# Moving up to three heads' columns of V in each weighted-sum matmul of a windowed attention

## The chip, the cores and the metric

The kernel runs on one core of one Trainium2 chip. The metric is the device time of one execution in microseconds (us), lower is better. A run's time is a little longer than the span of its profile, which reaches from the first to the last instruction.

## What is computed

The reference mixes two branches of a sequence of 2048 positions and 640 channels by a gate: a convolution as long as the sequence (done by FFT in the reference, by matmuls with constant matrices in the kernel), and an attention of 32 heads of 20 channels, where each position looks at 8 positions, 2 apart. The change lies in the last but one line of the attention:

```
x = A_q
g = _sigmoid((x * gate_w).sum(-1, keepdims=True))
a = _A_ref(x, A_k, A_v, A_shift_k, A_ssm_k, A_ssm_D)     # the long convolution
# _B_ref, the attention:
qkv = (x @ wqkv).reshape(B, S, 3, H, Dh)                  # H = 32, Dh = 20
idx = pos[:, None] - 2 * arange(8)[None, :]               # masked where idx < 0
logits = einsum("bhsd,bhswd->bhsw", q, kg) * scale
attn = softmax(logits)
o = einsum("bhsw,bhswd->bhsd", attn, vg)
return o.reshape(B, S, D) @ wo
# the result: g * a + (1 - g) * b
```

## The kernel before, in words

The sequence is split into even and odd positions, so that a window is 8 neighbours, and each half into 9 blocks of 114 queries, 18 blocks in all; a block's queries need 121 keys. The 32 heads are worked in 8 sets `t` of 4 heads. For one set there are these steps:

- `score_gen` (matmuls on L595, tile `sc`): for each block and head one matmul gives keys x queries, 121 x 114. A head's weights hold 31 rows, in one quarter of the array's rows, and two heads at a time stand in different quarters. The blocks are taken in five groups (4, 4, 4, 3, 3 blocks), each in two steps `k` of two heads, so a set has 10 steps, of 8 or 6 matmuls.
- ACT makes the exponentials of a step in one instruction (L602) and writes them to `ETall`, a ring of 8 buffers.
- `pv_gen` (L623, tile `O`): for each block and head the 121 x 128 block of `ETall` is loaded as weights and 21 columns of `VW` are moved through it: the 20 channels of V for that head and a column of ones, which gives the softmax's sum. A set has 72 such matmuls, 48 for the first 12 blocks and 24 for the last 6, each of the two parts in one go after all its exponentials. Within a part the loops run over groups, then heads (`hf`, `hh`), then blocks, so the four heads `h4 = 0..3` of a block follow one another in time. The results of the four heads of a block stand side by side in PSUM, 84 columns a block, 21 a head.
- DVE divides (L632, L635) into `oS`.

`VW` holds for each block all 32 heads side by side, 21 columns each, so neighbouring heads are neighbours in memory.

Around it, other work shares TensorE (PE) in an order that is written out by hand: the strings ORDER and ENGINES name, request by request, which generator issues next and whether ACT or DVE evicts. Four PSUM buffers of two banks go round. The projection of V (L478, all rows of the array, 320 columns) comes first and makes `VW`. Up to about 107 us the projections of Q and K (`pj`, L527, all rows, 342 or 349 columns) fill the places between the scores. After that the FFT's first steps on the filter do (`s1_unit`, L656, 64 rows x 128 columns moved; `s2_unit`, L672, 160 columns), until the attention's end at about 138 us; then come the same steps on the other operand, the transposes of `oS` (L790), the output projection (L810), the inverse transform (L772, L861) and the last products.

Of the kernel before, what the change touches and what calls it, by code (L numbers as in the profile page):

```python
# [26 lines left out]
BQ = 114  # L27
BK = 121
# [149 lines left out]
def kernel(  # L178
# [14 lines left out]
    nc = tc.nc  # L193
# [19 lines left out]
    def psum(g, name, shape=(128, 2, 512), dt=F32, k=0):  # L213
        t_ = psp.tile(list(shape), dt, name=name, tag=f"ps{g.banks[k]}")
        return t_
# [24 lines left out]
    VW = pR.tile([128, NB, H, DH + 1], BF, name="VW")  # L240
# [5 lines left out]
    ETall = pR.tile([128, NET, 2, 3 * BQ + 128], BF, name="ETall")  # L246
# [13 lines left out]
    def ev(name):  # L260
        if name not in E:
            E[name] = Ev()
        return E[name]

    def mark(name, g):
        x = ev(name)
        x.t, x.eng = g.done.t, g.done.eng
# [340 lines left out]
    def pv_gen():  # L608
        n = 0
        for t in range(NT):  # L610
            for gis, b0, na in PARTS:
                mm_ = sum(4 * len(GROUPS[gi]) for gi in gis)
                blocks = [b for gi in gis for b in GROUPS[gi]]
                g = yield Req("P", 28.0 * mm_ + 30.0, [ev(f"e{t}{gi}{k}") for gi in gis for k in range(2)] + [ev(f"VW{b}h{t // 4}") for b in blocks], take=1, mode="f", mm=mm_)
                O = psum(g, "O")
                for gi in gis:
                    for hf in range(2):
                        e = step[(t, gi, hf)]
                        for hh in range(2):
                            for bb, b in enumerate(GROUPS[gi]):  # L620
                                h4 = 2 * hf + hh
                                c0 = 84 * ((b - b0) % 6) + 21 * h4
                                nc.tensor.matmul(O[:, (b - b0) // 6, c0:c0 + 21], lhsT=ETall[0:BK, e, hh, BQ * bb:BQ * bb + 128],  # L623
                                                 rhs=VW[0:BK, b, 4 * t + h4, :], start=True, stop=True, skip_group_check=True)
                        x = etfree[e]
                        x.t, x.eng = g.done.t, "P"
                rd = rds[n % 2]
                n += 1
                r = yield Req("D", 150.0 + 7.0 * 24 * na + na * (140.0 + 1.055 * 480), [g.done], give=g.banks)
                Ov = O[0:BQ, 0:na, 0:504].rearrange("p a (b e) -> p a b e", e=21)  # L630
                rv = rd[0:BQ, 0:24 * na].rearrange("p (a b) -> p a b", a=na)
                nc.vector.reciprocal(rv, Ov[:, :, :, DH])  # L632
                for a in range(na):
                    dst = oS[0:BQ, b0 + 6 * a:b0 + 6 * a + 6, 80 * t:80 * t + 80].rearrange("p b (h d) -> p b h d", h=4)
                    nc.vector.tensor_tensor(dst, Ov[:, a, :, 0:DH].rearrange("p (b h) d -> p b h d", h=4),  # L635
                                            rv[:, a].rearrange("p (b h) -> p b h", h=4).unsqueeze(3).to_broadcast([BQ, 6, 4, DH]), ALU.mult)
        mark("oS", r)
        mark("pv", g)
# [246 lines left out]
    for gen in (loads, late, fragger, score_gen, pv_gen, conv, bulk, conv_v, conv_end, qkproj, gate, load_GT, h_slot, p2_slot,  # L885
                u_slot, swaps, op_tr, outproj, load_q, gate_q, final, stores):
        plan.add(gen())
# [34 lines left out]
```

## Time and profile before

| | |
|---|---|
| median of 3 runs | 231.96 us (230.49, 231.96, 232.22) |
| the profiled execution | 232.02 us |
| its span, first to last instruction | 229.9 us |
| mean granted TensorE clock over the span | 0.924 |
| weighted-sum matmuls (L623) | 576, busy 17.3 us, first at 54.0 us, last at 138.1 us |
| score matmuls (L595) | 576, busy 24.2 us |
| exponentials (L602) | 80, busy 63.8 us |

Busy times add up the durations of instructions. Matmuls are pipelined, so that one of them "lasts" 173 ns in the profile, while the next starts some 25 ns after it; the pace is read from the length of a run of matmuls, and not from one's duration. PEclk is the share of the full TensorE clock that was granted. A wait for several things is put down to the one that came last.

### The profile page before, as it was taken

To read this page: it belongs to the slowest core of one execution; us is meant where nothing else is said; L and a number is where in the kernel's file an instruction comes from. 1 tells how busy PE (TensorE), PEld (TensorE's weight loads), DVE (VectorE), ACT (ScalarE), POOL (GpSimd) and SP (SyncE) were. 2 spreads that over 40 slices of the span, in tenths; PEclk is the share of its full clock that TensorE was granted. 3 is DMA by queue.
4 is the path that set the end of the run, shared out by engine and by line. 5 is a ranking of instruction groups with operands and counts; after the bars stand their busy time and mean duration, and the time that the engine had idled before them with its cause. 6 is when DMAs were issued, how large, how long until landed. Compare 5 with 4: busy or idle time off the path is not lost.

```text
span 229.9 us, 8777 instructions
## 1 busy us (share of the span) xinstructions
PE 209.2 (91%) x3802; PEld 168.2 (73%) x3802; DVE 189.2 (82%) x259; ACT 165.3 (72%) x215; POOL 63.6 (28%) x144
## 2 busy tenths in 40 slices
PE   6859999999899999999898998999899999999940
PEld 2647978857656766566676788898798899998930
DVE  4353999779868989977997679999999998979990
ACT  2012535378498888587888879979999999788960
POOL 8891005945734754745500000000000000000000
PEclk9997999999999999999855557999999999999996
DMA  7999856869999999797797661096887955921872
GB/s 171 205 232 232 169 173 142 171 117 170 145 158 174 150 156 156 117 139 125 139 139 215 182 204 41 3 222 157 174 189 161 227 98 117 199 35 25 196 183 66
DMA packets 74742, 34.92 MB, mean 152 GB/s; under 512 B 58276, under 2 KB 71152, under 8 KB 74704
## 3 DMA queue, kind: packets, MB, share of 16 engines
q1 hardware_dynamic: 68896, 26.93, 61.3%
q0 software_dynamic: 4080, 6.41, 13.4%
q10 hardware_dynamic: 1728, 1.02, 1.7%
q8 instruction: 29, 0.48, 1.0%
q14 instruction: 9, 0.07, 0.1%
HBM read 18.43 MB, written 2.62 MB: 92 GB/s over the span
## 4 chain that ended last, share of the span: by engine, by line
PE 55%; DVE 18%; DMA 10%; POOL 5%; ACT 4%; issue 4%; SPq 2%; DVEq 0%; POOLq 0%; ACTq 0%
PE pj L527 13%; PE i L772 8%; PE psv L478 8%; PE op L810 6%; PE s L672 6%; PE sc L595 6%; DMA xT<-in_A_q_dram 5%; DVE Hs L207 4%; ACT ETall L602 4%; PE s L656 4%; PE O L623 4%; DMA kb<-stg 3%; DVE SX L873 3%; DVE SX L870 3%; DMA Dz<-in_A_ssm_D_dram 2%
## 5 line engine op out<-in xcount | busy, mean ns | idle before, releaser
L602 ACT ACTIVATE ETall<-sc 121x912 bf16<-121x912 f32 (+1 forms) x80 | 63.8, 858 | 10.5 <-PE sc L595 9.9
L527 PE MATMUL pj<-xT,Wqk 128*128 128x342 bf16 (+1 forms) x300 | 48.8, 312 | 0.3 <-DVE stg L207 0.3
L527 PEld LDWEIGHTS <-Wqk 128*128 128x128 bf16 x300 | 27.9, 98 | 15.0 <-issue 0.2
L205 ACT CAST UC<-s 128x960 bf16<-128x960 f32 (+2 forms) x32 | 29.4, 980 | 1.8 <-PE s L656 1.2
L478 PE MATMUL psv<-KX,xT 128*121 128x320 bf16 x180 | 27.1, 310 | 3.9 <-DMA xT<-in_A_q_dram 2.7
L478 PEld LDWEIGHTS <-xT 128*121 128x121 bf16 x180 | 24.8, 139 | 6.0 <-DMA xT<-in_A_q_dram 3.0
L572 POOL DMA_DIRECT2D qb<-stg x36 | 18.1, 505 | 35.6 <-ACT stg L205 21.8
L595 PE MATMUL sc<-qb,kb 31*128 31x114 bf16 x576 | 24.2, 232 | 2.3 <-ACT ETall L602 0.6
L436 DVE TENSOR_TENSOR KX<-KX 128x1760 bf16<-128x1760 bf16 (+1 forms) x24 | 24.6, 1042 | 0.4
L810 PE MATMUL op<-wo,oT 128*32 128x320 bf16 x640 | 24.0, 303 | 0.3 <-ACT SX L866 0.3
L205 ACT CAST VW<-psv 121x640 bf16<-121x640 f32 x13 | 8.9, 696 | 20.9 <-PE psv L478 20.9
L595 PEld LDWEIGHTS <-kb 31*128 31x128 bf16 x576 | 14.4, 101 | 12.3 <-issue 8.9
L672 PEld LDWEIGHTS <-SX 64*128 64x128 bf16 x512 | 20.5, 100 | 3.5 <-issue 2.8
L810 PEld LDWEIGHTS <-oT 128*32 128x32 bf16 x640 | 21.2, 140 | 1.4 <-issue 0.2
L205 ACT CAST stg<-pj 128x684 bf16<-128x684 f32 (+1 forms) x14 | 10.4, 742 | 16.4 <-PE pj L527 10.0
L572 POOL DMA_DIRECT2D kb<-stg x36 | 18.1, 507 | 11.6 <-DVE stg L207 5.6
L207 DVE CAST stg<-pj 128x726 bf16<-128x726 f32 (+1 forms) x16 | 14.3, 896 | 7.9 <-PE pj L527 4.7
L207 DVE CAST SX<-s 128x1024 bf16<-128x1024 f32 (+1 forms) x15 | 17.7, 1195 | 2.9 <-PE s L672 2.0
L443 DVE TENSOR_TENSOR KX<-KX 128x1760 bf16<-128x1760 bf16 (+1 forms) x18 | 18.8, 1043 | 0.4
L623 PEld LDWEIGHTS <-ETall 121*128 121x128 bf16 x576 | 16.4, 98 | 2.3 <-issue 1.2
L772 PE MATMUL i<-F,Hw 128*128 128x128 bf16 x160 | 18.0, 219 | 0.0
L772 PEld LDWEIGHTS <-Hw 128*128 128x128 bf16 x160 | 17.9, 114 | 0.0
(76 smaller groups left out, 350.7 us busy)
## 6 DMA issues: line engine op xcount, KB each, us to landing
vin<-in_A_v_dram SPq DMA_DIRECT2D x8, 320.0 KB
h_lin<-in_A_ssm_k_dram SPq DMA_DIRECT2D x16, 160.0 KB
Hw<-SX SPq DMA_DIRECT2D x8, 320.0 KB
Hw<-Hs SPq DMA_DIRECT2D x8, 320.0 KB
SX<-in_A_q_dram SPq DMA_DIRECT2D x16, 160.0 KB
kb<-stg POOLq DMA_DIRECT2D x28, 85.1 KB, 4.2
qb<-stg POOLq DMA_DIRECT2D x28, 80.2 KB, 4.3
SX<-cf_G SPq DMA_DIRECT2D x4, 512.0 KB
```

Of the source, the lines that this page charges most:

```text
L205: nc.scalar.copy(dst, src)
L207: nc.vector.tensor_copy(dst, src)
L436: eng.tensor_tensor(d, kin[:, n + 3 - j:n + 3 - j + m, :], w.to_broadcast([128, m, QC]), ALU.mult)
L478: nc.tensor.matmul(ps[0:BK, i, 0:320], lhsT=xT[:, dt, s0:s0 + BK], rhs=Wv[:, dt, 320 * hf:320 * hf + 320], start=(dt == 0), stop=(dt == ND ...
L527: nc.tensor.matmul(ps[:, i, 0:n], lhsT=Wqk[:, dt, w, 128 * ft:128 * ft + 128], rhs=xT[:, dt, s0:s0 + n], start=(dt == 0), stop=(dt == NDT ...
L572: nc.gpsimd.dma_start(dst[r0:r0 + rows, 0:wd], stg[fa - f0:fb - f0, 0:wd])
L595: nc.tensor.matmul(sc[:, hh, BQ * bb:BQ * bb + BQ], lhsT=kb[r:r + DH + NF, BK * b:BK * b + 128], rhs=qb[r:r + DH + NF, BQ * b:BQ * b + BQ] ...
L602: nc.scalar.activation(ETall[0:BK, e, :, 0:BQ * nb], sc[0:BK, :, 0:BQ * nb], ACT.Exp, scale=SCALE)
L623: nc.tensor.matmul(O[:, (b - b0) // 6, c0:c0 + 21], lhsT=ETall[0:BK, e, hh, BQ * bb:BQ * bb + 128], rhs=VW[0:BK, b, 4 * t + h4, :], start= ...
L672: nc.tensor.matmul(ps[:, c, 160 * jj:160 * jj + 160], lhsT=st["G"][rows, j0 + jj, rr, :], rhs=Am[rows, rr].rearrange("p o (q j) l -> p j ( ...
L772: nc.tensor.matmul(d, lhsT=st[(key, P)][:, c, o + il // 4, :, il % 4], rhs=M[:, k, :], start=(k == 0), stop=(k == 1), skip_group_check=True)
L810: nc.tensor.matmul(op[c:c + 32, tt, 0:320], lhsT=oT[:, ft, h, 32 * e:32 * e + 32, a], rhs=wo[:, ft, 320 * w:320 * w + 320], start=(ft == 0 ...
```

## The change

One statement of `pv_gen` is changed. The weights stay as they are; the moved columns are those of up to three neighbouring heads, beginning with the matmul's own: heads 0 and 1 of a set move 63 columns, head 2 moves 42 and head 3 moves 21 as before. The matmul of head 0 thus writes head 0's place and the two places to the right of it; these hold values of no use (head 0's weights times the V of heads 1 and 2), and the matmuls of heads 1, 2 and 3, which come later in the same part and start anew (`start=True`), write over them. What stands in PSUM at the end is the same. The number and the order of instructions on every engine are the same too, and no wait is added or removed.

```diff
                             for bb, b in enumerate(GROUPS[gi]):
                                 h4 = 2 * hf + hh
                                 c0 = 84 * ((b - b0) % 6) + 21 * h4
-                                nc.tensor.matmul(O[:, (b - b0) // 6, c0:c0 + 21], lhsT=ETall[0:BK, e, hh, BQ * bb:BQ * bb + 128],
-                                                 rhs=VW[0:BK, b, 4 * t + h4, :], start=True, stop=True, skip_group_check=True)
+                                nc.tensor.matmul(O[:, (b - b0) // 6, c0:c0 + 21 * min(3, 4 - h4)], lhsT=ETall[0:BK, e, hh, BQ * bb:BQ * bb + 128],
+                                                 rhs=VW[0:BK, b, 4 * t + h4:4 * t + min(4, h4 + 3), :].rearrange("p h e -> p (h e)"), start=True, stop=True, skip_group_check=True)
                         x = etfree[e]
                         x.t, x.eng = g.done.t, "P"
```

## The prediction

> **What bounds the kernel now.** I read the page's utilization and its slices first, then the granted clock by stages, then the chain of waits through the attention, and last the lines that share TensorE there.
>
> ```profile
> span 229.9 us, 8777 instructions
> PE 209.2 (91%) x3802; PEld 168.2 (73%) x3802; DVE 189.2 (82%) x259; ACT 165.3 (72%) x215; POOL 63.6 (28%) x144
> ...
> PEclk9997999999999999999855557999999999999996
> ...
> PE pj L527 13%; PE i L772 8%; PE psv L478 8%; PE op L810 6%; PE s L672 6%; PE sc L595 6%; DMA xT<-in_A_q_dram 5%; DVE Hs L207 4%; ACT ETall L602 4%; PE s L656 4%; PE O L623 4%; DMA kb<-stg 3%; DVE SX L873 3%; DVE SX L870 3%; DMA Dz<-in_A_ssm_D_dram 2%
> ```
>
> PE is occupied nearly throughout, and the chain that ended last, whose lines stand in the last row, is mostly PE. But in four of the 40 slices the granted clock is about half. By stages (columns: stage, length, busy time and count of PE, PEld, DVE, ACT, POOL, then the clock, DMA share, GB/s):
>
> ```profile
> 14.26:17.67 3.41, 1.30 (x10) 1.28 (x11) 1.87 (x3) 0.00 (x0) 3.41 (x4) 1.00 1.15 225
> 17.67:21.08 3.41, 3.41 (x14) 2.62 (x13) 0.30 (x1) 0.69 (x1) 0.69 (x1) 0.50 1.06 254
> ...
> 109.83:113.24 3.41, 3.02 (x92) 2.44 (x95) 3.07 (x4) 2.97 (x4) 2.76 (x10) 1.00 0.65 131
> 113.24:116.66 3.42, 3.11 (x53) 1.92 (x51) 3.24 (x5) 2.85 (x4) 0.00 (x0) 0.50 1.06 180
> ...
> 137.14:140.55 3.41, 3.41 (x74) 3.18 (x71) 3.34 (x5) 2.70 (x4) 0.00 (x0) 0.50 0.40 130
> 140.55:143.96 3.41, 2.70 (x70) 2.26 (x66) 3.41 (x4) 3.41 (x5) 0.00 (x0) 1.00 0.02 5
> ```
>
> The clock is a half exactly from 17.67 to 21.08 and from 113.24 to 140.55. The second is 27.31 us, eight times the first's 3.41. So it steps on a grid of 3.41 us, and I take it that the work of one stage decides the clock of the next. In the eight slow stages the chain of waits runs over PE:
>
> ```profile
> 107.61 0.33 PE sc L595 x8
> ...
> 110.20 0.35 PE s L656 x8
> ...
> 117.47 0.49 PE sc L595 x8
> 117.97 0.54 PE s L656 x8
> ```
>
> The same eight matmuls take 0.49 and 0.54 us there, against 0.33 and 0.35 before. ACT waits for PE in those stages:
>
> ```profile
> ACT ETall L602 <- PE sc L595: 3.7, 7, 1.0
> ACT Hs L205 <- PE s L656: 0.5, 2, 0.3
> ACT SX L205 <- PE s L672: 0.2, 1, 0.2
> ```
>
> **The change part by part.** No instruction, wait or DMA is added or moved. Of four matmuls of a block, two move 63 columns, one 42 and one 21: 189 in place of 84, 47.25 on average. Three things follow: the price at full clock, the price at half clock, and what the columns do to the clock.
>
> *At full clock.* Pace of the weighted sums (O) by runs of 48 and 24, and that of plain full-array matmuls:
>
> ```profile
> 108.61 0.76 PE L623 MATMUL O<-VW,ETall 121*128 121x21 bf16 x24
> ...
> 111.85 1.36 PE L623 MATMUL O<-VW,ETall 121*128 121x21 bf16 x48
> ```
>
> ```profile
> 44.84 2.91 PE pj L527 x20
> 187.42 17.99 PE i L772 x320
> ```
>
> (1.36 - 0.76)/24 = 25.0 ns a matmul of 21 columns. 128 columns take 17.99/320 = 56.2 ns, 342 take 2.91/20 = 145.5 ns, hence 0.417 ns a column, and 63 columns take 56.2 - 65 x 0.417 = 29.1 ns. 42 columns (20 ns) stay under the 25 ns. So half of the 576 matmuls cost 4.1 ns more: 288 x 4.1 = 1.2 us of PE. O has about 4% of the span on the chain (the page's row above), 9 us of its 576 x 25 ns = 14.4 us, so some 0.6 of it counts: 0.7 us, of which 0.5 in the 408 matmuls before 113 us. Bounds: 0 and 1.2; I take 0.6. [...]
>
> *At half clock.* The same runs there:
>
> ```profile
> 116.66 0.81 PE L623 MATMUL O<-VW,ETall 121*128 121x21 bf16 x24
> ...
> 122.06 1.45 PE L623 MATMUL O<-VW,ETall 121*128 121x21 bf16 x48
> ```
>
> (1.45 - 0.81)/24 = 26.7 ns, so 21 columns hardly feel the clock. 63 columns at twice 0.417 ns take 52.5 ns, 42 take 35. A run of 24 costs 12 x 25.8 + 6 x 8.3 = 0.36 us more. The slow stages hold 168 such matmuls, seven runs of 24: 2.5 us, if they all stay slow. ACT waits for PE there, so I charge it in full; half hidden behind the exponentials it would be 1.3.
>
> *The clock.* I measure a stage's work as moved columns times the share of the array's rows used (a quarter for sc, a half for s, all for O and pj), against 3.41 us / 0.417 ns = 8192 columns. Counts by line in the decisive stages, in the order L595, L656, L672, L623:
>
> ```profile
> 109.83:113.24 3.41, 1.12 (x28) 0.72 (x31) 1.00 0.65 131
> ...
> 120.07:123.48 3.41, 0.72 (x16) 0.26 (x14) 0.50 0.82 179
> ...
> 130.31:133.72 3.41, 0.65 (x16) 0.41 (x18) 0.50 0.50 151
> ```
>
> ```profile
> 109.83:113.24 3.41, 0.80 (x16) 0.45 (x16) 1.00 0.65 131
> ...
> 120.07:123.48 3.41, 1.22 (x16) 0.79 (x16) 0.50 0.82 179
> ...
> 137.14:140.55 3.41, 2.13 (x38) 1.73 (x35) 0.50 0.40 130
> ...
> 147.38:150.79 3.41, 3.03 (x56) 2.58 (x56) 1.00 0.46 95
> ```
>
> ```profile
> 130.31:133.72 3.41, 1.51 (x24) 1.19 (x18) 0.50 0.50 151
> ...
> 137.14:140.55 3.41, 1.01 (x12) 0.79 (x12) 0.50 0.40 130
> ```
>
> ```profile
> 109.83:113.24 3.41, 1.36 (x48) 1.27 (x48) 1.00 0.65 131
> ...
> 130.31:133.72 3.41, 1.45 (x48) 1.35 (x48) 0.50 0.50 151
> ...
> 137.14:140.55 3.41, 0.82 (x24) 0.72 (x24) 0.50 0.40 130
> ```
>
> Stage 109.83, after which the clock fell: 28 x 28.5 + 16 x 64 + 48 x 21 = 2830, a share of 0.35. Stage 14.26, after which it fell too: ten matmuls of 320 (L478), 0.39. Stage 147.38, which kept it: 56 x 64 = 3584, 0.44 or a little over. Stage 130.31, which did not bring it back: 456 + 24 x 80 + 1008 = 3384, 0.41. Stage 137.14, which did: 2432 + 960 + 504 = 3896, 0.48. One line between 0.41 and 0.44 fits all five.
>
> With the wider columns each O adds 26.25 columns. Stage 109.83 gets 48 x 26.25 = 1260 more: 0.50, so the clock stays. The stage behind it holds no run of 48. At full clock ACT sets its pace; from
>
> ```profile
> 102.32 1.37 ACT L602 ACTIVATE ETall<-sc 121x684 bf16<-121x684 f32 x2 [0.17 <-PE sc L595]
> ...
> 108.02 4.78 ACT L602 ACTIVATE ETall<-sc 121x912 bf16<-121x912 f32 x6 [0.18 <-PE sc L595]
> ```
>
> with the middle and the least duration of one, 926 and 735 ns,
>
> ```profile
> L602 ACT ACTIVATE ETall<-sc x80: 735/926/966, 48.1 to 135.5; 121x912 bf16<-121x912 f32 x48, 121x684 bf16<-121x684 f32 x32
> ```
>
> an exponential of 912 comes every (4.78 - 0.93)/5 = 0.77 us: 4.4 in a stage, with 35 sc (1000), three s units (1536) and a run of 24 O (24 x 47.25 = 1134): 3670, 0.45, hardly above the line, and a little slack puts it below. I expect the clock to fall there, one stage later than now. Stage 130.31 at half clock gets 1260 more, less 0.73 us (two runs) of its other work, 0.21 x 2376 = 510: 0.50, so the clock comes back at 133.7 and not at 140.55. That is five slow stages in place of eight. Stage 120.07, with 48 O too, gets 456 + 1024 + 2268 - 0.21 x 1480 = 3437, 0.42, and may do it earlier.
>
> What a slow stage costs: the waits of ACT for PE, 3.7 + 0.5 + 0.2 = 4.4 us in eight, 0.55 each. Above, with the one other instruction that ACT has in such a set,
>
> ```profile
> 121.81 1.01 ACT L205 CAST SX<-s 128x1024 bf16<-128x1024 f32 x1
> ```
>
> a set needs 6 x 0.77 + 4 x 0.64 (1.37 - 0.73) + 1.0 = 8.2 us of ACT, but the runs of 48 O begin at 111.85 and 122.06, 10.2 apart: 2.0 a set, 5.4 in 2.7 sets. Below: half the waits, 2.2, since ACT waited 0.2 us at full clock too. Behind the stage the gain is kept, for what comes next waits for this stage's own results: the transfers of L758, which the products need, stood waiting for DVE's copy of a tile that PE finished in it.
>
> ```profile
> SPq L758 <- DVE SX L207: 9.3, 1, 9.3
> ```
>
>
> *Sum*, with five slow stages, which hold 144 O (six runs of 24): 0.6 + 6 x 0.36 - 3 x 0.55 = +1.1 us. The profiled execution took 232.02 us, 0.06 over the median, so 233.1 us against its time and 233.0 against the median. The loss is odd: more full clock, but dearer matmuls while it lasts.
>
> **The rivals.** (1) *The clock never falls*, or for at most a stage or two: 0.7 - 4.4 = -3.7, 228.3 us (down to 227.3 with the upper bound of 5.4). For it: stage 109.83 passes clearly, the one behind lies at 0.45. It also follows if the clock counts the time that any column moves, without the rows: then the stages of scores weigh more. Against it: the rows with half rows used, 0.44 kept and 0.41 not brought back, fit one line only with the rows counted. It decides where the stage behind 113.24 holds more than the line.
>
> (2) *Slower: the clock does what it did*, eight slow stages, and the wide matmuls pay the half clock: 0.5 + 2.5 = +3.0, 235.0 us; with half hidden 233.8. It decides where stage 130.31 stays under the line, as it would if wide rows were not what is counted. [...]
>
> (3) *The columns cost nothing and do nothing*: within 0.3 us of 232. It asks that the slow stages' O hide wholly, against ACT's waits there.
>
> **How the numbers follow.** Five slow stages, or four to seven (0.6 + 1.8 - 2.2 = +0.2 to 0.6 + 2.5 - 0.55 = +2.6; 232.2 to 234.6): 0.49. Rival 1: 0.27. Rival 2: 0.19. Rival 3: 0.05. A measurement of this kernel can tell about 1% from no change, 2.3 us. Rival 1 is faster by more: 0.27. Slower by more than 1% (over 234.3) are most of rival 2 and the top of the first case, 0.21 together. The rest, 0.52, is within 1%. The range takes in rival 1 at its middle and rival 2: 227.9 to 235.2 us; the likeliest case alone has 232.2 to 234.6. Forecast: 233.0 us.
>
> **What would show it.** In the changed profile: runs of 48 O of about 1.46 us at full clock (1.36 now) and 2.2 us at half clock (1.45 now); a clock that falls one stage later, and comes back two earlier. If O's runs at full clock are no longer, the first term is nil. If no stage after 107 us is slow, rival 1 is right; if there are eight again, rival 2. A stage with less than 0.41 by my count that keeps the clock would show my measure of work wrong.

## The result, and the profile after

| | before | changed |
|---|---|---|
| median of 20 runs each | 231.91 us | 231.45 us |
| lowest and highest | 229.80, 235.17 us | 227.01, 234.82 us |
| the profiled execution, its span | 232.02, 229.9 us | 230.49, 228.4 us |
| its mean granted TensorE clock | 0.924 | 0.951 |

The ratio to before is 0.9895, with a 95% interval from 0.985 to 0.994. It compares, of each kernel, the runs within 1.5% of its fastest; for the changed kernel these are 5 of 20, runs with little half clock, so that the ratio shows its good runs and the medians (0.2% apart) show the usual one. The means, 231.85 and 231.14 us, differ by 0.7 us, which the scatter of the runs (standard deviations of 1.4 and 1.8 us) does not set clear of no change. The forecast was 233.0 us, a loss.

The spread is part of the result. The clock records of both profiles hold 1.00 and 0.50 alone, so from a run's span and mean clock follows its time at half clock, 2 x (1 - clock) x span. In the changed kernel it is 20.0 us on average (5.4 to 29.3 in 20 runs), and the run's time goes with it: a straight line through the 20 runs rises by 0.24 us for each us at half clock, with a correlation of 0.86. In 29 runs of the kernel before on another occasion it is 33.2 us (22.1 to 39.3). Some 8.5 us of it lie at the start and behind the last matmul, to judge by e5 and e7 below, whose profiles have no other (5.4 to 10.5 us in their 12 runs). By that the changed kernel has some 3.4 slow stages of 3.41 us on average, and the kernel before 7.2.

The page of the changed kernel, its span and the granted clock in 40 slices. In the middle two slices stand at 5 and one at 7, in place of four at 5 with an 8 and a 7 beside them in the row before:

```profile
span 228.4 us, 8777 instructions
...
PEclk9799999999999999999975599999999999999995
```

Its stages of 3.41 us (stage, length, busy time and count of PE, PEld, DVE, ACT, POOL, then clock, DMA share, GB/s):

```profile
113.79:117.21 3.42, 2.85 (x72) 2.14 (x71) 3.39 (x6) 3.42 (x6) 0.00 (x0) 1.00 1.09 186
117.21:120.62 3.41, 3.32 (x54) 2.07 (x52) 3.41 (x4) 3.18 (x4) 0.00 (x0) 0.50 1.33 135
...
127.44:130.86 3.42, 3.42 (x54) 2.58 (x52) 2.65 (x3) 3.15 (x4) 0.00 (x0) 0.50 0.66 192
130.86:134.27 3.41, 3.06 (x95) 2.60 (x93) 2.30 (x4) 2.62 (x5) 0.00 (x0) 1.00 0.60 185
```

The clock is at half from 117.21 to 130.86, four stages in place of eight. It falls one stage later, as forecast, and returns three earlier, where two were forecast. The runs of weighted sums (O) in the changed kernel, from set 5 on, in order of time:

```profile
111.38 1.46 PE L623 MATMUL O<-VW,ETall 121*128 121x63 bf16 x48
115.84 0.81 PE L623 MATMUL O<-VW,ETall 121*128 121x63 bf16 x24
120.94 2.19 PE L623 MATMUL O<-VW,ETall 121*128 121x63 bf16 x48
125.55 1.19 PE L623 MATMUL O<-VW,ETall 121*128 121x63 bf16 x24
131.59 1.46 PE L623 MATMUL O<-VW,ETall 121*128 121x63 bf16 x48
136.00 0.81 PE L623 MATMUL O<-VW,ETall 121*128 121x63 bf16 x24
```

A run of 48 takes 1.46 us at full clock, 0.10 more than before, and 2.19 at half clock, 0.74 more than the 1.45 before. The last of the kernel before was

```profile
137.47 0.82 PE L623 MATMUL O<-VW,ETall 121*128 121x21 bf16 x24
```

In what follows "the stretch" is the time from the start of set 5's first O to the end of the last one. Before: 111.85 to 138.29, 26.4 us. Changed: 111.38 to 136.81, 25.4 us. So of the 1.53 us between the two profiled executions 1.0 was gained in the stretch, and 0.5 was there when it began; behind the last O both need 91.6 us to the end of the span. The beginning of the kernel differs by such amounts between all profiles here (set 5 starts between 109.9 and 112.2 us where the scores are issued once), with no order in the width of the columns.

### The profile page after: what moved, and what is told of

It is laid out like the page before. It is cut to its first block, busy times and chain, and to the rows that moved or that the text cites. A ratio compares the mean times of both kernels' runs of the same rounds, so it can differ in the third digit from the quotient of the medians.

```text
span 228.4 us, 8777 instructions
## 1 busy us (share of the span) xinstructions
PE 205.9 (90%) x3802; PEld 166.9 (73%) x3802; DVE 188.3 (82%) x259; ACT 164.9 (72%) x215; POOL 63.2 (28%) x144
## 4 chain that ended last, share of the span: by engine, by line
PE 51%; DVE 19%; DMA 12%; ACT 5%; issue 4%; POOL 3%; SPq 2%; DVEq 0%; ACTq 0%; POOLq 0%
PE pj L527 13%; PE i L772 8%; PE psv L478 7%; PE op L810 6%; PE s L672 5%; DMA xT<-in_A_q_dram 5%; DMA kb<-stg 5%; PE sc L595 4%; PE O L623 4%; ACT ETall L602 4%; DVE Hs L207 4%; DVE SX L873 3%; DVE SX L870 3%; DVE UC L207 3%; DMA Dz<-in_A_ssm_D_dram 2%
## 5 line engine op out<-in xcount | busy, mean ns | idle before, releaser
L478 PE MATMUL psv<-KX,xT 128*121 128x320 bf16 x180 | 27.3, 311 | 4.0 <-issue 2.2
L205 ACT CAST UC<-s 128x960 bf16<-128x960 f32 (+2 forms) x32 | 29.3, 979 | 2.1 <-PE s L656 1.6
L595 PE MATMUL sc<-qb,kb 31*128 31x114 bf16 x576 | 22.8, 224 | 3.5 <-DMA kb<-stg 1.5
L595 PEld LDWEIGHTS <-kb 31*128 31x128 bf16 x576 | 13.7, 98 | 12.9 <-issue 8.6
L672 PEld LDWEIGHTS <-SX 64*128 64x128 bf16 x512 | 19.3, 96 | 3.7 <-issue 2.9
L623 PEld LDWEIGHTS <-ETall 121*128 121x128 bf16 x576 | 18.4, 99 | 2.1 <-issue 0.7
L623 PE MATMUL O<-VW,ETall 121*128 121x63 bf16 (+2 forms) x576 | 19.3, 189 | 0.4 <-ACT ETall L602 0.3
```

What stands on the lines that cost most here:

```text
L205: nc.scalar.copy(dst, src)
L478: nc.tensor.matmul(ps[0:BK, i, 0:320], lhsT=xT[:, dt, s0:s0 + BK], rhs=Wv[:, dt, 320 * hf:320 * hf + 320], start=(dt == 0), stop=(dt == ND ...
L595: nc.tensor.matmul(sc[:, hh, BQ * bb:BQ * bb + BQ], lhsT=kb[r:r + DH + NF, BK * b:BK * b + 128], rhs=qb[r:r + DH + NF, BQ * b:BQ * b + BQ] ...
L623: nc.tensor.matmul(O[:, (b - b0) // 6, c0:c0 + 21 * min(3, 4 - h4)], lhsT=ETall[0:BK, e, hh, BQ * bb:BQ * bb + 128], rhs=VW[0:BK, b, 4 * t ...
L672: nc.tensor.matmul(ps[:, c, 160 * jj:160 * jj + 160], lhsT=st["G"][rows, j0 + jj, rr, :], rhs=Am[rows, rr].rearrange("p o (q j) l -> p j ( ...
```

## The experiments

The theory to test (1): a stage of 3.41 us in which the moved columns, weighted by the rows they use, fill less than a certain share halves the clock of the next, and the wide columns act by lifting that share. The share, some 0.39, is the author's estimate from the profiles before and after (stage 113.79 of the changed kernel lost the clock with 0.37, and 106.97 kept it with 0.40, as counted further below). Rivals: (2) any moving column counts, without the rows; (3) the clock follows gaps of PE; and, on the time, that wide matmuls gain or cost in every set alike.

**e1_early: wide columns where the clock is safe.** `nh` stands for the number of heads moved.

```diff
+                                nh = min(3, 4 - h4) if t < 5 else 1
```

> Wide columns (63, 63, 42, 21) in the head sets 0 to 4 only, 21 columns in sets 5 to 7, so that nothing is changed in the stretch where the clock falls. Theory 1 (a stage of 3.41 us in which the moved columns, weighted by the share of the array's rows that they use, fill less than about 0.39 of the array's time halves the clock of the next; wide columns act only by lifting that share): as many slow stages after 107 us as before, 6 to 8, and a time within 0.3% of before; the first O of set 5 no more than 0.5 us later than before's 102.2 us. Rival (the gain comes from the wide matmuls themselves, in every set): five eighths of the changed kernel's gain.

231.30 us, ratio 0.9987 (0.995 to 1.0023). Half clock in 12 runs: 32.7 us, before 33.2. Slices of the clock, and the stretch's first and last O:

```profile
PEclk9999999999999999999655559999999999999995
```

```profile
109.88 1.43 PE L624 MATMUL O<-VW,ETall 121*128 121x21 bf16 x48
...
135.62 0.82 PE L624 MATMUL O<-VW,ETall 121*128 121x21 bf16 x24
```

The stretch is 26.6 us with its eight slow stages, as before. So wide columns in the sets 0 to 4 gain nothing, and cost nothing that can be measured. (The expectation takes the run at 102.2 us for set 5's first; it is set 4's. Set 5 begins at 111.85.)

**e2_late: wide columns in the sets 5 to 7 only.**

```diff
+                                nh = min(3, 4 - h4) if t >= 5 else 1
```

> Wide columns in the head sets 5 to 7 only. Theory 1: the same slow stages as the changed kernel, 3 to 6, beginning one stage later or ending earlier than before; a time within 0.3% of the changed kernel's, which varies from run to run by some 3% with where the grid of 3.41 us falls. Rival (wide matmuls gain in every set): three eighths of the changed kernel's gain.

232.04 us, ratio 1.0074 (1.002 to 1.0129), but the medians are only 0.2% apart (231.62 before). So a loss is not clear, and a gain is not there, although half clock falls to 26.0 us from 33.2.

```profile
111.53 1.45 PE L624 MATMUL O<-VW,ETall 121*128 121x63 bf16 x48
116.17 1.19 PE L624 MATMUL O<-VW,ETall 121*128 121x63 bf16 x24
121.94 2.19 PE L624 MATMUL O<-VW,ETall 121*128 121x63 bf16 x48
126.55 1.19 PE L624 MATMUL O<-VW,ETall 121*128 121x63 bf16 x24
...
137.39 0.81 PE L624 MATMUL O<-VW,ETall 121*128 121x63 bf16 x24
```

The clock is at half from 115.67 to 132.74, five stages, as the expectation allows. What would be four runs of 24 now pay the half clock (1.19, 2.19, 1.19), and the stretch is 26.7 us against 26.4 before: three fewer slow stages are just eaten by the dearer matmuls. The changed kernel itself does the same in its second profile (e8 below), so the narrow sets 0 to 4 need not be the reason. The median is within 0.3% of the changed kernel's 231.45, measured on another occasion; the half clock is longer than its 20.0 us. The run of set 4 ahead of the stretch, narrow here, may be why in some runs: 24 narrow O would take the share of stage 106.97 of the changed kernel (counted below) from 0.40 to 0.32. No run shows this.

**e3_four: 84, 63, 42 and 21 columns.**

```diff
+                                nh = 4 - h4
```

> All four heads of the set from a head on: 84, 63, 42, 21 columns, 52.5 on average in place of 47.25. Theory 1: a run of 48 O adds 252 columns to a stage, 0.03 of its time, and stages just under the line pass: 2 to 4 slow stages on average, 0.5 to 1 us faster than the changed kernel. Rival (the price decides): 84 columns take 35 + 3 = 38 ns at full clock, 9 more than 63, 0.1 us a run of 48, and 70 ns at half clock, 0.2 us a run of 48: 0.5 to 1 us slower than the changed kernel.

231.71 us, ratio 0.9978 (0.9942 to 1.0014); 20.9 us at half clock, as with three heads. The count of slow stages is as expected, but the gain of 0.5 to 1 us is not there, nor the rival's loss; no run of the changed kernel stood beside it. More columns in the O runs did not save more stages: the stage that lets the clock fall (113.27 in its profile) has only the last 11 O of a run of 48 in it. The stretch with five slow stages:

```profile
112.15 1.56 PE L624 MATMUL O<-VW,ETall 121*128 121x84 bf16 x48
116.72 1.28 PE L624 MATMUL O<-VW,ETall 121*128 121x84 bf16 x24
122.59 2.39 PE L624 MATMUL O<-VW,ETall 121*128 121x84 bf16 x48
...
138.45 0.86 PE L624 MATMUL O<-VW,ETall 121*128 121x84 bf16 x24
```

27.2 us, with 2.39 for 48 at half clock.

**e4_scores_twice: columns on a quarter of the rows.** O is narrow.

```diff
-                            nc.tensor.matmul(sc[...], ...)
+                            for rep in range(2 if t >= 5 else 1):
+                                nc.tensor.matmul(sc[...], ...)
```

> O as before with 21 columns; in the sets 5 to 7 every score matmul is issued twice into the same place. It adds 72 x 114 columns a set, on a quarter of the rows: 2052 columns when weighted by rows, about what the wide columns add (72 x 26.25 = 1890), but 8208 when rows are not counted. Theory 1 (rows counted): slow stages still come after 107 us, 3 to 7. Rival 2 (any moving column counts): two score matmuls run side by side, so the share of time with columns moving rises by some 0.3 in every stage and no stage after 107 us is slow. Rival 3 (the clock follows gaps of TensorE alone): eight slow stages or a number that has nothing to do with the columns.

238.43 us, ratio 1.0285 (1.0222 to 1.0349). Stages of it:

```profile
110.77:114.18 3.41, 3.02 (x101) 2.56 (x94) 2.74 (x3) 3.08 (x4) 2.27 (x9) 1.00 0.67 146
114.18:117.60 3.42, 3.24 (x75) 2.70 (x72) 2.81 (x4) 1.96 (x3) 0.00 (x0) 0.50 1.12 194
...
141.49:144.90 3.41, 3.41 (x70) 3.01 (x72) 2.50 (x3) 2.94 (x4) 0.00 (x0) 0.50 0.02 5
144.90:148.31 3.41, 2.57 (x67) 1.96 (x65) 3.38 (x5) 3.22 (x5) 0.00 (x0) 1.00 0.00 0
```

The clock is at half from 114.18 to 144.90, nine stages. Theory 1 expected 3 to 7; the stretch itself is longer here, 31.7 us. The added columns, on a quarter of the rows, did not hold the clock. Counts of scores and of the filter's second step (L595 and L672 of the kernel before) in one of the slow stages:

```profile
131.25:134.66 3.41, 2.02 (x48) 1.54 (x42) 0.50 0.49 154
```

```profile
131.25:134.66 3.41, 1.59 (x22) 1.28 (x24) 0.50 0.49 154
```

Without the rows that is 48 x 114 + 22 x 160 = 8992 columns, and the clock stayed at half. Stage 127.44 of the changed kernel, whose rows stand further below, has 16 x 114 + 38 x 160 = 7904, and the clock came back. Counted as time in which any column moves (at half clock twice the 0.417 ns a column) it is 0.88 of this stage against 0.84 there. (Two scores do run side by side: one after the other, eight of 114 columns at twice 0.417 ns would take 0.76 us, and the eight at 117.47 before took 0.49.) So rival 2 is out. Rival 3 allows nine stages, but no rival of gaps fits here or in the prediction's stages: PE was busy 3.02 of 3.41 us in the stage ahead of the fall, and 2.57 in one that held the clock.

**e5_wide_s1, e6_s1_only, e7_late_s1: more columns between the O runs.** The same trick on the filter's first step, whose results also stand side by side:

```diff
-                nc.tensor.matmul(ps[:, qp, 128 * il:128 * il + 128], lhsT=lhsT, rhs=F1b[rows, :], start=True, stop=True,
+                w = 256 if key == "h" and il < 3 else 128
+                nc.tensor.matmul(ps[:, qp, 128 * il:128 * il + w], lhsT=lhsT, rhs=F[rows, 0:w], start=True, stop=True,
```

e5 has it on top of the changed kernel, e6 without wide O, and e7 with wide O from the second run of set 4 on (`nh = min(3, 4 - h4) if (t, b0) >= (4, 12) else 1`).

> The changed kernel, and in the FFT's first step on the filter (L656, half of the array's rows, two matmuls side by side) three of four matmuls move 256 columns in place of 128, the second 128 being written over by the next ones: 384 more full columns in each unit of eight matmuls, two or three units in a stage, 0.09 to 0.14 of its time. Theory 1 (row-weighted columns set the clock, about 0.39 is needed): every stage after 107 us passes, no slow stage or one in the stretch from the first O of set 5 to the last O; that stretch, 26.2 us before and 25.2 in the changed kernel, falls to 21 to 22.5, and the time to 227 to 228.5, with less spread. Rival (the wider columns' price eats the gain at full clock too): the stretch stays over 24.5 us though no stage is slow.

> Weighted sums with 21 columns as before; only the FFT's first step on the filter is widened, as in the run beside it. Theory 1: stages with three units pass, those with an O run and two units or fewer do not; 3 to 7 slow stages in the stretch, time within 1% of before, and a spread as wide as the changed kernel's. Rival (wide weighted sums are needed as such): as before, seven or eight slow stages.

> As the first of these, with the wide columns of the weighted sums only from the second run of set 4 on (108.6 us before), the last ones before the stretch where the clock falls. Theory 1: no slow stage in the stretch, the same time as the first of these within 0.3%. Rival (wide columns in the earlier sets cost full-clock time): up to 0.5 us faster than it.

e5: 228.67 us, ratio 0.987 (0.9829 to 0.9912), half clock 9.0 us. Its clock and its stretch:

```profile
PEclk9997999999999999999999999999999999999996
```

```profile
111.19 1.45 PE L623 MATMUL O<-VW,ETall 121*128 121x63 bf16 x48
...
133.29 0.81 PE L623 MATMUL O<-VW,ETall 121*128 121x63 bf16 x24
```

No stage between 107 us and the last matmul is slow, and the stretch is 22.9 us, 3.5 less than before; the guess was 21 to 22.5, and 227 to 228.5 for the time. This is what the whole of the half clock was worth, with the price at full clock of all the added columns in it.

e7: 228.20 us, ratio 0.9856 (0.982 to 0.9893), half clock 8.3 us, in its profile none of it before the last matmul; six runs from 227.28 to 229.03, where before had 229.93 to 233.92 in 17.

```profile
110.49 1.45 PE L624 MATMUL O<-VW,ETall 121*128 121x63 bf16 x48
...
132.58 0.81 PE L624 MATMUL O<-VW,ETall 121*128 121x63 bf16 x24
```

22.9 us again. e7 is 0.5 us faster than e5, as its rival allows, but their runs overlap, so that a price of the wide columns before the stretch is neither shown nor excluded. e7's slowest run beats the fastest of those 17, and its median is 3.5 us under that of the changed kernel (e8).

e6: 232.37 us, ratio 1.0008 (0.9969 to 1.0047), half clock 27.3 us (16.4 to 33.4 in 12 runs). Before had 33.9 us at half clock. The filter's columns alone take away some of the slow stages, and pay for it while the rest lasts:

```profile
111.08 1.35 PE L623 MATMUL O<-VW,ETall 121*128 121x21 bf16 x48
...
138.50 0.76 PE L623 MATMUL O<-VW,ETall 121*128 121x21 bf16 x24
```

28.2 us with seven slow stages. So with other columns than O's the time at half clock was shorter too, 27.3 us against 33.9, but with these alone the clock still fell; e5 and e7 have both.

**e8_changed_again: the changed kernel beside those three.**

> The changed kernel once more, on the same chip as the three others. Theory 1: a mean of about three slow stages in the stretch, seven before; mean time 0.2 to 1 us under before, single runs from 227 to 235 us.

231.69 us median, 227.10 to 232.29 in six runs, against 231.81 before (229.93 to 233.92); ratio 0.9869 (0.9787 to 0.9952), of the same kind as in the result above. Half clock 21.6 us, before 33.9. The median hardly moves, the mean is 1.1 us lower (0.2 to 1 was expected, and the scatter of six runs does not set it clear of no change), and the lowest run is 2.8 us under the lowest before. Its profile, of a run of 231.65 us, is a second one of the changed kernel:

```profile
PEclk9997999999999999999955599999999999999995
```

```profile
111.40 1.46 PE L623 MATMUL O<-VW,ETall 121*128 121x63 bf16 x48
116.05 1.19 PE L623 MATMUL O<-VW,ETall 121*128 121x63 bf16 x24
121.83 2.19 PE L623 MATMUL O<-VW,ETall 121*128 121x63 bf16 x48
126.44 1.19 PE L623 MATMUL O<-VW,ETall 121*128 121x63 bf16 x24
132.85 1.46 PE L623 MATMUL O<-VW,ETall 121*128 121x63 bf16 x48
```

The clock is at half from 115.44 to 132.50, five stages, and the stretch is 26.7 us, 0.2 more than before.

## Why the prediction was wrong

*The bound, and the mechanism*: right in the main, as far as the counts of this case go. A stage's clock went with the row-weighted columns of the stage before it, by the shares counted below; that they decide it is the author's reading of these counts. e4 speaks against leaving out the rows: 8992 columns without the rows left the clock at half there, and 7904 in stage 127.44 of the changed kernel came ahead of its return. Against gaps speaks stage 14.80 of the changed kernel, which kept the clock with PE busy 1.80 of 3.41 us, while stage 113.79 lost it with 2.85. Of the 13 matmuls of 320 columns on all rows that its row counts 11 begin in it, a share of 0.43:

```profile
14.80:18.21 3.41, 1.80 (x13) 1.49 (x12) 1.19 (x2) 0.00 (x0) 3.32 (x2) 1.00 1.13 219
18.21:21.63 3.42, 3.42 (x27) 2.91 (x26) 1.71 (x2) 0.95 (x2) 0.00 (x0) 1.00 1.11 260
```

In the changed kernel's profile, counts by line in the order L595, L656, L672, L623 (stage 127.44 has none of L656 and L623):

```profile
106.97:110.38 3.41, 1.77 (x38) 1.03 (x38) 1.00 0.36 83
...
113.79:117.21 3.42, 1.60 (x32) 0.96 (x31) 1.00 1.09 186
...
127.44:130.86 3.42, 1.12 (x16) 0.64 (x16) 0.50 0.66 192
```

```profile
106.97:110.38 3.41, 0.80 (x16) 0.45 (x16) 1.00 0.36 83
...
113.79:117.21 3.42, 0.70 (x16) 0.46 (x16) 1.00 1.09 186
```

```profile
127.44:130.86 3.42, 2.57 (x38) 1.94 (x36) 0.50 0.66 192
```

```profile
106.97:110.38 3.41, 0.81 (x24) 0.80 (x24) 1.00 0.36 83
...
113.79:117.21 3.42, 0.81 (x24) 0.71 (x24) 1.00 1.09 186
```

With 47.25 columns for an O: stage 106.97, which kept the clock, holds 1083 + 1024 + 1134 = 3241 of 8192, 0.40; stage 113.79, which lost it, 912 + 1024 + 1134 = 3070, 0.37; stage 127.44, which brought it back, 456 + 3040 = 3496, 0.43. But such a row also counts matmuls that began in the stage before, and at half clock that weighs:

```profile
127.19 0.98 PE L672 MATMUL s<-SX 64*128 64x160 bf16 x12
...
130.00 1.40 PE L672 MATMUL s<-SX 64*128 64x160 bf16 x24
```

Of the 38 of L672 six began before 127.44; with 32 the stage holds 456 + 2560 = 3016, 0.37. The prediction's line rests on the same slip: six of the 24 of L672 in its stage 130.31 began earlier, so that this stage holds 0.35 and not 0.41, and stage 137.14 holds 0.43 and not 0.48. Counted by starts in all ten profiles, from 105 us to the last O, every stage at full clock that lost it has 0.30 to 0.375, and every one that kept it 0.39 or more. At half clock those that brought it back have 0.37 to 0.43, and those that did not have up to 0.39. One line at some 0.38 to 0.39, an estimate from these counts, fits all of them but two at half clock (this one, and a stage of e6 with 0.388 that did not bring it back); the prediction had 0.41 to 0.44.

*Price at half clock*: a run of 48 costs 0.74 us more, 0.73 forecast. *Price at full clock*: 0.10 us a run of 48 (1.46 us, 1.36 before), as forecast (24 x 4.1 ns). Whether 0.6 us of it reach the end is not shown. From the first O of set 0 to that of set 5 the profile before takes 57.8 us, the changed kernel 58.4 and 57.3, e1, e3 and e5 with wide columns 57.8, 57.5 and 57.5, but e2 and e6 with narrow ones 57.2 and 58.3: the scatter is larger than the term.

*What a slow stage costs*: 0.55 us forecast; e5 loses eight and gains 3.5 us in the stretch with the wide columns' price in it, so 0.44 or more. Right in size.

*The count of stages, and the O in them*: this is the step that failed, "five slow stages, which hold 144 O". In the changed kernel's first profile it is four, and they hold 72 O: the run of 24 at 115.84 was through before the fall, and that of 48 at 131.59 came after the return. With its own prices, and without the 0.6, the sum would have been 3 x 0.36 - 4 x 0.55 = -1.1 us, and the stretch measured -1.0. In the second profile (e8) it is five, as forecast, but they hold 96 O: 4 x 0.36 - 3 x 0.55 = -0.2 us, and the stretch measured +0.2.

The O that are missing are the 48 of set 7. The prediction had them bring the clock back, at stage 130.31, and pay the half clock meanwhile. In all four profiles with wide columns in the stretch and a clock that falls (these two, e2 and e3) the clock was back before that run began, and the stage that brought it back holds no O at all: only 32 to 36 matmuls of L672 and 12 or 16 scores, a share of 0.37 once and 0.39 three times. So wide columns in that stage did not bring the clock back; by the count it hung on how much of the filter's second step the grid of 3.41 us put into one stage. With narrow columns the nearest such stages did not bring it back (34 and 16 in e6, 0.39; 30 and 21 before, 0.37). Whether the wide columns had a part in this is not shown.

The fall came where it was forecast, partly by luck. By the count the wide columns kept the clock in the stage before: 110.38, with 48 O, holds 0.46 by starts, and would hold 0.31 with 21 columns. But the forecast put 0.45 into the next one, over its own line, and had it fall by "a little slack"; the stage holds 0.37, with two units of L656 in place of three.

Moreover the forecast worked with one position of the grid. It differs between the profiles (the clock fell at 117.21 us in the first of the changed kernel and at 115.44 in the second, 1.77 apart), and with it the work that falls into one stage; the time at half clock of the changed kernel goes from 5 to 29 us. So the sign hung on one stage and one run of 48.

Rival 1 is what the best runs do (227.01 us, with 5.4 us at half clock, less than the ends alone take on average); rival 2 is neither of the changed kernel's two profiles. Rival 3 is near the medians, but by a gain and a price that cancel, and not because neither is there.

What stays open: the position of the grid was not set by any experiment, only read from profiles; why the clock came back a stage or more earlier with wide columns than with narrow ones; and why the beginnings of the runs differ by up to 2 us.

## What to carry to other kernels

Look at the granted clock by stages before counting instructions: where it falls though TensorE is hardly idle, columns moved for nothing can be worth their price, as in e5 and e7 (228.67 and 228.20 us, before 231.81). Here such columns paid only where they kept the clock up throughout; half a cure made the remaining slow stages dearer (2.19 us for a run of 48, 1.45 before), and the median did not move. Put them where the stages are empty (here between the weighted sums), and judge by many runs, for the grid of the stages lay differently from profile to profile (1.77 us between the changed kernel's two).

## What the runs showed of the hardware

The granted clock changed in steps of 3.41 us: ahead of the last matmul it was at half for 3.41 and 27.31 us in the profile before, and for 3.41 and 13.65 us in the changed kernel's. It fell after stages where PE was busy 2.85 (changed) and 3.02 us (before) of 3.41, and stayed up after one with 1.80 (changed). As moved columns weighted by the rows in use, of 8192 a stage, counted by starts in ten profiles from 105 us to the last O: stages at full clock that lost it had 0.30 to 0.375, and those that kept it 0.39 or more; at half clock those that brought it back had 0.37 to 0.43, and those that did not up to 0.39. Ahead of 105 us, stage 14.26 before lost it with 0.39, and stage 14.80 of the changed kernel kept it with 0.43. Doubling the columns of matmuls on a quarter of the rows left nine stages slow (e4). Weighted sums of 21 columns ran at 25.0 ns at full and 26.7 ns at half clock, nearly the same (before); a run of 48 with 63, 63, 42 and 21 columns took 1.46 and 2.19 us (changed).
